# Linear attention before a mixture of experts: units of two heads of two sequences in place of four heads of one sequence with tails

## The chip, the core and the metric

The program runs on one core of a Trainium2 chip. TensorE (PE, with its weight loads listed apart as PEld) multiplies and transposes, VectorE (DVE) and ScalarE (ACT) do elementwise work and read PSUM, GpSimd (POOL) does elementwise work in SBUF and issues gathers, and the queue of SyncE (SP) issues most transfers. Each engine works through its own instructions in the order in which they were written down, and waits on semaphores. The metric is the device time of one execution in microseconds; lower is better. All arithmetic here is float32, which TensorE does in two passes, so that one matmul of the kernel is two records in the trace.

## What is computed

Attention without a softmax over pairs: `q` is normalised over its 64 features, `k` over the 576 positions, and a 64x64 matrix per head carries everything. Its output goes into a gated mixture of eight experts (two per token), and from there through a dense feed-forward layer.

```python
batch, n_heads, seq, head_dim = (4, 8, 576, 64)
q_s = softmax(q, axis=-1); k_s = softmax(k, axis=2)        # eps 1e-9 in the sums
kv = einsum('bhsd,bhse->bhde', k_s, v)
x = einsum('bhsd,bhde->bhse', q_s, kv)                     # -> (2304, 512)
logits = x @ w_gate
noisy = logits + log1p(exp(x @ w_noise)) * noise           # top 2 of 8 experts per token
out[token] += weight * (relu(x @ w1[e]) @ w2[e])           # 512 -> 1024 -> 512
h = out @ w_in; g = max(h, 0) + alpha * min(h, 0); result = g @ w_out
```

## The kernel before

The program has three stages: attention (to about 120 us), the experts, and the last layer. The second and third are one almost unbroken stream of matmuls, and the change leaves their code alone, but for which PSUM banks they share with attention and for the order of the output rows.

**Units.** Attention works in eight units. A unit is one sequence and four heads. Its first 512 positions lie on 128 partitions, four rows each (`"h (p c) d -> p h (c d)", c=4`), and so each run of memory in a load is 1 KB. The remaining 64 positions of each sequence are its tail. The tails of two sequences share one tile, one on each half of the partitions (`kt`, `vtr`, `qt`; runs of 256 bytes), and have instructions of their own: `k_tail`, `k_tail_exp`, a second part in `q_max`, `q_sub`, `q_exp`, `v_copy`, a fifth matmul in `kv_mm` (`et`, `vt`), and a third piece (`cc == 2`) of `q_tr`, `x_mm`, `x_out`.

**Steps of a unit.** `k_tree` (DVE) takes the maximum of `k` over a partition's rows, `k_tr` (PE) transposes that, `k_bc` reduces it over the partitions (DVE) and transposes the maximum back (PE), `k_row` (ACT) copies it to SBUF, `k_sub` (POOL; DVE for the first two units) subtracts, `k_exp` (ACT) takes the exponential. `q_max` (DVE), `q_sub` (POOL), `q_exp` (ACT) do the same for `q`. `v_copy` (POOL) puts a column of ones beside `v`. `kv_mm` (PE) multiplies, `kv_sum` (DVE, tile `rk`) and `kv_out` (ACT) normalise, `kv_tr` (PE and ACT, tile `kvt`) transposes the result and `kv_gate` multiplies it by the gate weights, so that the logits come out of the same matmul as the output. `q_tr` (PE, and ACT's copy to `qT`) transposes exp(q), `x_mm` (PE) multiplies into the PSUM tile `px`, `x_out` (DVE) normalises output and logits and sums the logits over the heads, `x_st` (SP) stores.

**Order.** Nothing reorders instructions. The loop `for t in range(-6, NU)` calls `slot(t)`, and a slot runs through the table `ORDER`: an entry `("kv_mm", 1)` does `kv_mm` of unit t+1. That table is the order of every engine's queue. Below, slot 0 is the one in which `x_mm` of unit 0 runs.

**Routing beside it.** The gate of the first half of the tokens (`gate`, a generator of some forty small DVE instructions with groups of PE matmuls in between) runs within slots 4 to 7: each `tick()` behind a DVE instruction of attention takes `TICKS[t]` steps of it. When it has ended, `fetch` puts four gathers of tokens (`xg`) into POOL's queue. `SPLITS` says at which entries of the table a piece of the first expert's weights is split into a high and a low part (`hi` on ACT, L165; `lo` on POOL, L166).

**The end of the stage.** In the last slot, at the entry `TURNED`, PE transposes two gathered blocks of tokens into PSUM tiles `pt`, ACT copies them to `xh`, and DVE forms `xl` from `pt` and `xh` at `SPLIT`. Then the first expert's matmuls begin (L755). Their accumulators take the banks `mm0` to `mm4` in turn, `mm0` first. Before, `pt` uses the banks `mm1` and `mm2`:

```python
for c, tag in enumerate(("mm1", "mm2")):
    pt = gps.tile([128, 4, 128], F32, name="pt", tag=tag)
```

Of the kernel before, what the change touches and what calls it, by code (L numbers as in the profile page):

```python
# [18 lines left out]
NT = 18  # L19
# [7 lines left out]
EPS = 1e-9  # L27
NVA = 2
NKV = 6
# [6 lines left out]
ORDER = [("k_tree", 3), ("x_mm0", 0), ("q_sub", 2), ("x_out0", 0), ("kv_mm", 1), ("k_tail", 2), ("k_exp", 2),  # L36
         ("kv_sum", 1), ("q_tr0", 1), ("k_tr", 3), ("x_mm2", 0), ("x_mm1", 0), ("k_bc", 3), ("kv_out", 1),
         ("k_tail_exp", 2), ("x_out2", 0), ("kv_tr", 1), ("q_tr1", 1), ("k_row", 3), ("x_st2", 0),
         ("load_k", 5), ("kv_gate", 1), ("q_max", 3), ("q_exp", 2), ("v_copy", 3), ("k_sub", 3), ("x_out1", 0),
         ("x_st0", 0), ("x_st1", 0), ("q_tr2", 1), ("load_v", 4), ("load_q", 5)]  # L40
# [12 lines left out]
def attention_moe_ffn(ctx, tc, q, k, v, w_gate, w_noise, noise, w1, w2, w_in, w_out, alpha, out):  # L53
# [126 lines left out]
    def attention():  # L180

        with ExitStack() as cx:
# [12 lines left out]
            vt = [att.tile([128, H, D + 1], F32, name=f"vt{i}") for i in range(2)]

            def main_src(a, b, g):
                return a[b, 4 * g:4 * g + 4, 0:512, :].rearrange("h (p c) d -> p h (c d)", c=4)

            def load(a, b, g, name):  # L200
                t = loads.tile([128, 4, 4, D], F32, name=name, bufs=3)
                nc.sync.dma_start(t.rearrange("p h c d -> p h (c d)"), main_src(a, b, g))
                return t
# [917 lines left out]
```

## Time and profile before

| | us |
|---|---|
| median of 3 runs (lowest, highest) | 995.41 (993.7, 996.4) |
| time of the profiled execution | 998.39 |
| its span, first to last instruction | 996.6 |
| PE busy, weight loads busy | 953.0, 860.0 |
| DVE, ACT, POOL busy | 508.0, 317.3, 307.0 |

A busy share is a mean over stages. PE is busy for 96% of the span, but for less in attention, and only there does it wait for others. To follow a change in attention, read the stretches of that stage (when the `x_mm` of each slot starts), and whether anything behind it has room. [...] The profiled execution is 3 us longer than the median, 1.8 us of its time lie outside the span.

### The profile page before, as it was taken

How to read it: one execution, taken by the hardware profiler on the slowest of the kernel's cores; microseconds unless marked ns; L12 is line 12 of the kernel's file. 1: busy time of each engine (PE TensorE's matmuls, PEld its weight loads, DVE VectorE, ACT ScalarE, POOL GpSimd, SP SyncE). 2: the span in 40 equal slices, each digit the busy share in tenths (PEclk: the TensorE clock that was granted, in tenths of full speed). 3: DMA queues.
4: the chain of work that ended last, by engine and by line, in shares of the span. 5: the costliest groups of instructions: out<-in, count | busy, mean ns of one | idle time of the engine just before them, and what ended most of it. 6: DMA issues, size and time to landing. Idle time of an engine off the chain costs nothing. (4 is left out here: it accounts for less than half of the span.)

```text
span 996.6 us, 14925 instructions
## 1 busy us (share of the span) xinstructions
PE 953.0 (96%) x5882; PEld 860.0 (86%) x5882; DVE 508.0 (51%) x1005; ACT 317.3 (32%) x603; POOL 307.0 (31%) x333
## 2 busy tenths in 40 slices
PE   4876799999999999999999999999999999999998
PEld 3765689998989898898988998989898989989896
DVE  6777563666757666666623354425161524334150
ACT  3554423433334333333333343212121222212120
POOL 6662730022212231312100127533251424323140
PEclk9986799999999999999999999999999999999999
DMA  9871643657656675756444262310101010100000
GB/s 251 247 215 54 213 146 124 191 164 239 192 184 205 181 240 162 244 171 200 149 136 136 81 200 70 88 51 14 53 15 61 15 50 22 43 22 11 11 12 21
DMA packets 65168, 121.77 MB, mean 122 GB/s; under 512 B 13488, under 2 KB 30400, under 8 KB 65088
## 3 DMA queue, kind: packets, MB, share of 16 engines
q1 hardware_dynamic: 49120, 83.98, 28.0%
q0 software_dynamic: 6080, 19.67, 6.4%
q10 hardware_dynamic: 9888, 17.08, 4.6%
q8 instruction: 48, 0.79, 0.3%
q14 instruction: 32, 0.26, 0.1%
HBM read 92.65 MB, written 28.05 MB: 121 GB/s over the span
## 5 line engine op out<-in xcount | busy, mean ns | idle before, releaser
L755 PE MATMUL mm<-xh,hi 128*128 128x256 f32 (+1 forms) x1088 | 318.4, 293 | 1.6 <-PEq L1080 0.9
L755 PE MATMUL mm<-xh,lo 128*128 128x256 f32 (+1 forms) x1088 | 318.3, 293 | 0.0
L755 PE MATMUL mm<-xl,hi 128*128 128x256 f32 (+1 forms) x1088 | 318.3, 293 | 0.0
L755 PEld LDWEIGHTS mm<-xh,hi 128*128 128x128 f32 x1088 | 205.8, 189 | 3.2 <-issue 1.3
L755 PEld LDWEIGHTS mm<-xl,hi 128*128 128x128 f32 x1088 | 205.3, 189 | 0.8
L755 PEld LDWEIGHTS mm<-xh,lo 128*128 128x128 f32 x1088 | 205.0, 189 | 0.0
L943 POOL TENSOR_TENSOR gl<-neg,gh 128x256 fp32r<-128x256 f32 x144 | 107.3, 750 | 166.1 <-ACT gh L942 164.8
L166 DVE TENSOR_TENSOR lo<-raw,hi 128x1024 fp32r<-128x1024 f32 x69 | 84.5, 1229 | 107.5 <-ACT hi L165 106.9
L940 DVE TENSOR_SCALAR neg<-mm,alph 128x256 f32<-128x256 f32 x144 | 69.2, 482 | 126.7 <-PE mm L755 124.7
L755 PE MATMUL mm<-hi,hh 128*128 128x512 f32 (+1 forms) x320 | 129.1, 403 | 0.0
L755 PE MATMUL mm<-hi,hl 128*128 128x512 f32 (+1 forms) x320 | 125.8, 393 | 0.0
L755 PE MATMUL mm<-lo,hh 128*128 128x512 f32 (+1 forms) x320 | 125.8, 393 | 0.0
L833 POOL TENSOR_TENSOR cva<-cva,raw 128x512 int32<-128x512 int32 x32 | 43.9, 1371 | 235.1 <-DVE raw L831 137.2
L755 PE MATMUL mm<-hi,gh 128*128 128x512 f32 x288 | 113.6, 394 | 0.0
L755 PE MATMUL mm<-hi,gl 128*128 128x512 f32 x288 | 112.3, 390 | 0.0
L755 PE MATMUL mm<-lo,gh 128*128 128x512 f32 x288 | 112.1, 389 | 0.0
L942 ACT CAST gh<-neg 128x256 fp32r<-128x256 f32 x144 | 57.6, 406 | 126.8 <-DVE neg L941 119.9
L780 ACT ACTIVATE hh<-mm 128x368 fp32r<-128x368 f32 (+1 forms) x128 | 54.9, 431 | 129.1 <-PE mm L755 119.7
L165 ACT CAST hi<-raw 128x1024 fp32r<-128x1024 f32 x80 | 83.2, 1047 | 28.0 <-DMA raw<-in_moe_w_dram 10.8
L781 DVE SCALAR_TENSOR_TENSOR hl<-mm,hh 128x368 fp32r<-128x368 f32 (+1 forms) x128 | 60.7, 479 | 57.8 <-ACT hh L780 57.4
L848 POOL DMA_INDIRECT xg<-ys,yidx x36 | 34.6, 962 | 157.8 <-DMA ys<-y 83.5
L709 DVE TENSOR_TENSOR xl<-pt,xh 128x512 fp32r<-128x512 f32 (+1 forms) x58 | 39.3, 678 | 69.2 <-ACT xh L706 68.9
(157 smaller groups left out, 1117.4 us busy)
## 6 DMA issues: line engine op xcount, KB each, us to landing
raw<-in_moe_w_dram SPq DMA_DIRECT2D x60, 512.0 KB, 3.9
ys<-y ACTq DMA_DIRECT2D x32, 256.0 KB, 2.0
raw<-in_moe_w_in_dram SPq DMA_DIRECT2D x16, 512.0 KB, 4.6
wc<-cvm SPq DMA_DIRECT2D x32, 256.0 KB, 4.9
raw<-in_moe_w_out_dram SPq DMA_DIRECT2D x16, 512.0 KB, 4.3
raw<-wc SPq DMA_DIRECT2D x16, 512.0 KB, 3.9
kr<-in_k_dram SPq DMA_DIRECT2D x8, 512.0 KB, 6.8
qr<-in_q_dram SPq DMA_DIRECT2D x8, 512.0 KB, 8.4
```

Source lines behind the costliest of these rows:

```text
L165: nc.scalar.copy(r(hi[:, sl]), raw)
L166: lo_eng.tensor_sub(r(lo[:, sl]), raw, hi[:, sl])
L709: nc.vector.tensor_sub(r(lo), pt, hi)
L755: nc.tensor.matmul(acc, r(a), r(b), start=(n, k) == steps[0], stop=(n, k) == steps[-1])
L780: nc.scalar.activation(r(hh[:, f, :]), acc[:, :n], AF.Relu)
L781: nc.vector.scalar_tensor_tensor(r(hl[:, f, :]), acc[:, :n], 0.0, hh[:, f, :], op0=OP.max, op1=OP.subtract)
L833: nc.gpsimd.tensor_tensor(a, a, low, op=OP.add)
L848: nc.gpsimd.indirect_dma_start(out=t, out_offset=None, in_=src, in_offset=bass.IndirectOffsetOnAxis(ap=yidx[:, i, T:T + 1], axis=0))
L940: nc.vector.tensor_scalar(t, a, 0.0, alph[:, f:f + 1], op0=OP.min, op1=OP.mult)
L942: nc.scalar.copy(r(GT[0][:, f, :]), t)
L943: nc.gpsimd.tensor_sub(r(GT[1][:, f, :]), t, GT[0][:, f, :])
```

## The change

A unit becomes two heads of two sequences. The sequence `2*hb` lies on partitions 0 to 63 and `2*hb + 1` on 64 to 127, with nine rows on each partition, 9 x 64 = 576. No tails remain. Runs of memory are 2304 bytes; a load is two transfers, one per half. There are again eight units.

- `kv_mm`: 18 matmuls a unit with 64 contraction rows each (two halves of nine rows), in place of 10 with 128 rows. The halves go to two PSUM banks.
- `x_mm`: 18 matmuls with 64 output partitions each, in place of 8 with 128 (and 4 with 64 in every second sequence), all into one tile `px` of three banks, of which there is one in place of two.
- `k_tr`, `k_bc`: two transposes a unit in place of six. The maximum is first spread by ACT (`kb`) and then transposed once.
- `x_out`: four DVE instructions a unit in place of five for each piece. `x_lg` sums the logits, on POOL, but for the last unit of each half of the tokens, where two adds are on DVE. `route` and its add fall away.
- `x_st`: three transfers of 384 KB every second unit.
- `ORDER`, `TICKS`, `SPLITS` are new; `kv_mm` stands one unit further ahead (2 in place of 1), `load_v` too. `pt` of the turned blocks uses `mm0` and `mm1`.
- `kv` has three buffers in place of six; noise is loaded in four transfers in place of eight; `out_rows` follows the new order of tokens.

```diff
-TICKS = {4: 1, 5: 2, 7: 3}
-SPLITS = {4: {"load_q": 1}, 5: {"load_q": 1}, 6: {"kv_mm": 1, "x_out1": 1, "load_q": 1},
-          7: {"kv_mm": 1, "x_out1": 1, "load_q": 1}}
+ORDER = [("x_mm", 0), ("k_tree", 3), ("k_exp", 2), ("q_sub", 2), ("kv_tr", 1), ("x_out", 0), ("q_tr0", 1), ("k_tr", 3),
+         ("kv_gate", 1), ("kv_mm", 2), ("k_bc", 3), ("q_tr1", 1), ("kv_sum", 2), ("k_row", 3), ("kv_out", 2),
+         ("load_k", 5), ("v_copy", 3), ("q_tr2", 1), ("q_max", 3), ("q_exp", 2), ("k_sub", 3), ("x_lg", 0),
+         ("x_st", 0), ("load_v", 5), ("load_q", 5)]
+TICKS = {4: 2, 5: 3, 6: 3, 7: 3}
+SPLITS = {4: {"load_q": 1}, 5: {"load_q": 1}, 6: {"kv_tr": 1, "k_bc": 1, "load_q": 1},
+          7: {"kv_tr": 1, "k_bc": 1, "load_q": 1}}
-TURNED, SPLIT = "x_st2", "load_q"
+TURNED, SPLIT = "kv_mm", "load_q"
...
+                t = loads.tile([128, 2, R * D], F32, name=name, bufs=3)
+                for u in range(2):
+                    nc.sync.dma_start(t[halves[u]], a[2 * hb + u, 2 * g:2 * g + 2].rearrange("h (p c) d -> p h (c d)", c=R))
...
+                kb = att.tile([128, 2, 64], F32, name="kb", bufs=2)
+                nc.scalar.copy(kb, km[:, :, None].to_broadcast([128, 2, 64]))
+                nc.tensor.transpose(pk[i][:, 1, :], kb.rearrange("p u n -> p (u n)"), ident)
...
+                p = pkv[i] = ps.tile([128, 2, 512], F32, name="pkv")
+                e = ek.pop(i)
+                for c in range(R):
+                    for u, h in enumerate(halves):
+                        nc.tensor.matmul(p[:, u, 0:130], e[h, c, :], va[i % NVA][h, :, c, :],
+                                         start=(c == 0), stop=(c == R - 1))
...
+                for c in range(R):
+                    for u, h in enumerate(halves):
+                        nc.tensor.matmul(px[i][h, c // 3, c % 3, :], t[:, c, h], m[:, u, :], start=True, stop=True)
...
-                nc.vector.reduce_sum(lgp[:, T:T + n, g, :], lt.rearrange("p c h n -> p c n h"), axis=AX.X)
...
+            def x_lg(i):
+                hb, g = divmod(i, G)
+                lt, at = lts.pop(i), lg[:, hb * R:(hb + 1) * R, :]
+                eng = nc.vector if g == G - 1 else nc.gpsimd
+                eng.tensor_add(at, lt[:, :, 0, :] if g == 0 else at, lt[:, :, int(g == 0), :])
+                if g:
+                    eng.tensor_add(at, at, lt[:, :, 1, :])
...
-                            for c, tag in enumerate(("mm1", "mm2")):
+                            for c, tag in enumerate(("mm0", "mm1")):
```

PE's queue in slot 1, from its first `x_mm` (`px`) to the last row ahead of the next slot's; `pkv` is `kv_mm`, `pq` is `q_tr`, `pk` are `k_tr` and `k_bc`, `bank` are `kv_tr` and `kv_gate`. Before (its `kv_132` is that of the unit of the slot):

```order
L395 MATMUL px<-kv_132,qT 128x162 x4
L332 MATMUL pkv<-va_141,ek 128x130 x4
L334 MATMUL pkv<-vt_143,et_139 128x130
L332 MATMUL pkv<-va_141,ek 128x130 x4
L334 MATMUL pkv<-vt_143,et_139 128x130
L379 MATMUL pq<-ident,eq 128x128 x4
L254 MATMUL pk<-ident,kt 128x128 x2
L256 MATMUL pk<-ident,m_436 128x128 x2
L395 MATMUL px<-kv_132,qT 128x162 x4
L265 MATMUL pk<-ident,km 128x128 x2
L357 MATMUL bank<-ident,kv_133 128x128 x2
L379 MATMUL pq<-ident,eq 128x128 x4
```

The same slot now (`kv_131` is that of its unit):

```order
L320 MATMUL px<-kv_131,qT 64x162 x18
L291 MATMUL bank<-ident,kv_132 128x128 x2
L310 MATMUL pq<-ident,eq 128x128 x3
L225 MATMUL pk<-ident,m_456 128x128
L298 MATMUL bank<-wg,kvt 128x16 x2
L271 MATMUL pkv<-va_134,ek 128x130 x18
L233 MATMUL pk<-ident,kb 128x128
L310 MATMUL pq<-ident,eq 128x128 x6
```

Before, a second `x_mm`, of the other two rows of the unit, stood between `kv_mm` and the next slot's first; now `x_mm` is one block, `kv_mm` stands behind `kv_tr` and `kv_gate`, and between it and the next `x_mm` PE has one transpose and six of `q_tr`.

DVE's queue at the end of the stage, from the last `x_out` on. Before:

```order
L408 TENSOR_TENSOR x<-px,rq_1238 128x512
L413 TENSOR_TENSOR lt_1243<-px,rq_1238 128x128
L417 TENSOR_REDUCE lgp<-lt_1243 128x2x16
L709 TENSOR_TENSOR xl<-pt,xh 128x4x128 x2
L478 TENSOR_TENSOR lg<-lgp 128x144
```

Now:

```order
L332 TENSOR_TENSOR x<-px,rq 128x9x128
L338 TENSOR_TENSOR lt<-px,rq 128x288
L347 TENSOR_TENSOR lg<-lg,lt 128x144
L349 TENSOR_TENSOR lg<-lg,lt 128x144
L625 TENSOR_TENSOR xl<-pt,xh 128x4x128 x2
```

The add of the logits stood behind `xl`, and two adds stand ahead of it now.

POOL's queue in the last two slots, now (`lo` are pieces of the first expert's weights, `xg` the gathers, `lg` the `x_lg` of unit 6):

```order
L166 TENSOR_TENSOR lo_886<-raw,hi_885 128x1024 x2
L604 DMA xg<-xs,tok_106 128x512 x4
L166 TENSOR_TENSOR lo_886<-raw,hi_885 128x1024
L347 TENSOR_TENSOR lg<-lg,lt 128x144
L349 TENSOR_TENSOR lg<-lg,lt 128x144
L166 TENSOR_TENSOR lo_1141<-raw,hi_1140 128x1024 x4
```

Before, four pieces stood between the last `et` and the gathers, and three behind them. Now two pieces stand ahead of the gathers, and the two adds of unit 6 stand behind the third.

## Rows read from the trace of the kernel before

**Rows 1.** Busy time by stretch; columns: stretch, its length, busy time per engine, PEclk, DMA share, GB/s
```profile
24.50:66.60 42.10, 34.78 (x244) 31.31 (x244) 28.98 (x69) 23.92 (x56) 26.43 (x20) 0.92 0.90 257
66.60:79.40 12.80, 8.35 (x57) 7.41 (x57) 12.47 (x33) 6.33 (x16) 7.31 (x6) 0.92 0.26 84
79.40:98.00 18.60, 11.93 (x90) 10.84 (x90) 11.89 (x38) 7.76 (x16) 6.97 (x4) 0.68 0.10 34
98.00:120.20 22.20, 16.05 (x94) 13.36 (x93) 13.18 (x47) 9.98 (x19) 15.44 (x9) 0.73 0.76 233
120.20:996.60 876.40, 870.90 (x5349) 789.15 (x5349) 426.22 (x804) 260.18 (x481) 235.22 (x254) 1.00 0.35 112
```

**Rows 2.** PE by time: start, length, line, tiles, records, idle before and releaser
```profile
15.88 1.94 PE L332 MATMUL pkv<-va,ek 128*128 128x130 f32 x8
...
38.37 0.38 PE L256 MATMUL pk<-ident,m 128*128 128x128 f32 x2
38.59 1.27 PE L395 MATMUL px<-kv,qT 128*128 128x162 f32 x8
39.70 0.38 PE L265 MATMUL pk<-ident,km 128*128 128x128 f32 x2
...
43.48 1.05 PE L332 MATMUL pkv<-va,ek 128*128 128x130 f32 x8
44.37 0.39 PE L334 MATMUL pkv<-vt,et 128*128 128x130 f32 x2
...
117.21 2.27 PE L705 MATMUL pt<-ident,xg 128*128 128x128 f32 x8 [2.73 <-DMA xg<-xs,tok]
120.15 1.23 PE L755 MATMUL mm<-xh,hi 128*128 128x256 f32 x4 [0.68 <-ACT xh L706]
```

**Rows 3.** POOL by time: a copy of `v`, and the first gather
```profile
46.68 1.04 POOL L319 COPY va<-vr 128x1024 f32<-128x1024 f32 x1 [7.67 <-DMA vr<-in_v_dram]
...
113.19 1.14 POOL L688 DMA_INDIRECT xg<-xs,tok  x1 [0.18 <-issue]
```

**Rows 4.** All engines by time in slot 5
```profile
81.78 2.35 POOL L166 TENSOR_TENSOR lo<-raw,hi 128x1024 fp32r<-128x1024 f32 x1 [0.33 <-ACT hi L165]
...
82.09 2.13 DVE L565 TENSOR_TENSOR gu<-gnl,gm 128x72 f32<-128x72 f32 x1
84.09 1.90 POOL L304 TENSOR_TENSOR eq<-qr,qm 128x1024 f32<-128x1024 f32 x1
84.25 1.82 DVE L567 TENSOR_TENSOR gu<-gu,rev 128x72 f32<-128x72 f32 x1
...
87.67 0.22 PE L581 MATMUL bank<-mask,tri 128*128 128x72 f16 x1 [5.70 <-DVE mask L576]
```

**Rows 5.** DVE by time: an add of logits with POOL idle
```profile
120.74 0.30 DVE L478 TENSOR_TENSOR lg<-lgp 128x144 f32<-128x144 f32 x1
```

**Rows 6.** DVE by form, 0 to 120 us; columns: shapes, count, busy us, mean ns, idle before
```profile
L244 DVE TENSOR_REDUCE m<-kr 128x256 f32<-128x1024 f32 x8 | 15.5, 1940 | 5.5 <-DMA kr<-in_k_dram 5.5
L408 DVE TENSOR_TENSOR x<-px,rq 128x512 f32<-128x512 f32 x16 | 11.0, 688 | 0.6 <-DMA xs<-x 0.2
L274 DVE TENSOR_REDUCE qm<-qr 128x16 f32<-128x1024 f32 x8 | 9.7, 1209 | 0.0
```

**Rows 7.** Weight loads of PE by time: 64 columns wide, then 128
```profile
62.41 0.47 PEld L395 LDWEIGHTS px<-kv,qT 128*64 128x64 f32 x8 [0.17 <-issue]
63.11 1.13 PEld L395 LDWEIGHTS px<-kv,qT 128*128 128x128 f32 x8 [0.23 <-issue]
```

**Rows 8.** ACT by form, 0 to 120 us
```profile
L350 ACT ACTIVATE kv<-pkv,rk 64x64 f32<-64x64 f32 x32 | 9.9, 309 | 1.8 <-DVE rk L341 1.4
L381 ACT COPY qT<-pq 128x512 f32<-128x512 f32 x16 | 9.4, 585 | 17.0 <-PE pq L379 16.5
```

**Rows 9.** POOL by form, 0 to 120 us
```profile
L285 POOL TENSOR_TENSOR ek<-kr,ks 128x1024 f32<-128x1024 f32 x6 | 14.2, 2374 | 10.1 <-ACT ks L269 7.8 <-DVE m L244 1.6 <-DMA nz<-in_moe_noise_dram 0.6
L291 POOL TENSOR_TENSOR et<-kt,ks 64x256 f32<-64x256 f32 x8 | 5.8, 723 | 0.3
```

More of the change, by code (lines that the diff above doesn't have):

```diff
@@ L27 @@
 EPS = 1e-9
+R = S // 64
 NVA = 2
-NKV = 6
+NKV = 3
 TG = 2
@@ L195, in attention @@
[L195 to L202, printed above, removed]
-                return t
-            def tail(a, hb, name):
-                t = loads.tile([128, H, D], F32, name=name, bufs=2 if name == "kt" else 1)
-                for u in range(2):
-                    nc.sync.dma_start(t[u * 64:(u + 1) * 64],
-                                      a[2 * hb + u, :, 512:576, :].rearrange("h p d -> p h d"))
-                return t
@@ L398, in x_out @@
-            def x_out(i, cc):
-                b, g = units[i]
-                T = 9 * (b // 2) + (8 if cc == 2 else 4 * (b % 2) + 2 * cc)
-                p, n = px.pop((i, cc)), 1 if cc == 2 else 2
-                rq = att.tile([128, n, 2, 2], F32, name=f"rq{n}", bufs=3)
+                m, t, p = kv[i % NKV], kvt.pop(i), bank[:, 256:288].rearrange("p (u n) -> p u n", u=2)
+                for u in range(2):
+                    nc.tensor.matmul(p[:, u, :], t[:, u, :], wg[:, i % G, :], start=True, stop=True)
@@ L440, in small_loads @@
                 for b in range(B):
-                    T, u = 9 * (b // 2) + 4 * (b % 2), b % 2
-                    nc.sync.dma_start(nz[:, T:T + 4, :],
-                                      noise[b * S:b * S + 512].rearrange("(p c) e -> p c e", c=4))
-                    nc.sync.dma_start(nz[u * 64:(u + 1) * 64, 9 * (b // 2) + 8, :],
-                                      noise[b * S + 512:(b + 1) * S])
-                nc.sync.dma_start(al, alpha.rearrange("(c p) -> c p", p=128))
-            def thirds(fn):
-                return [lambda i, cc=cc: (cc < 2 or units[i][0] % 2) and fn(i, cc) for cc in range(3)]
-            ops = {f.__name__: f for f in (load_k, load_q, load_v, v_copy, k_tree, k_tr, k_bc, k_row, k_sub, k_tail,
-                                           k_exp, k_tail_exp, q_max, q_sub, q_exp, kv_mm, kv_sum, kv_out, kv_tr,
-                                           kv_gate)}
-            for name, fn in (("q_tr", q_tr), ("x_mm", x_mm), ("x_out", x_out), ("x_st", x_store)):
-                ops.update((f"{name}{cc}", f) for cc, f in enumerate(thirds(fn)))
+                    nc.sync.dma_start(nz[halves[b % 2], b // 2 * R:(b // 2 + 1) * R, :],
+                                      noise[b * S:(b + 1) * S].rearrange("(p c) e -> p c e", c=R))
+                nc.sync.dma_start(al, alpha.rearrange("(c p) -> c p", p=128))
+            ops = {f.__name__: f for f in (load_k, load_q, load_v, v_copy, k_tree, k_tr, k_bc, k_row, k_sub, k_exp,
+                                           q_max, q_sub, q_exp, kv_mm, kv_sum, kv_out, kv_tr, kv_gate, x_mm, x_out,
+                                           x_lg, x_st)}
+            ops.update((f"q_tr{t}", lambda i, t=t: q_tr(i, t)) for t in range(3))
             def slot(t):
@@ L506, in attention @@
                 load_piece(queue=nc.scalar)
-            second = route(9, NT)
+            second = gate(R, NT)
             next(second)
```

244 lines of the change are left out of this document (80 added, 164 removed).

## The prediction

> **What bounds the kernel now.** I read the busy times by stretch first [rows 1]. From 120.2 us to the end PE is busy for 870.9 of 876.4 us at full clock. The change leaves that work alone, so the tail moves as a block with its first matmul, and what I have to predict is when the first expert matmul (L755) starts: now at 120.15 us [rows 2]. In front of it PE is never full: 34.8 of 42.1 us in slots 0 to 3, 8.35 of 12.8 in slot 4, 11.9 of 18.6 in slot 5, 16.05 of 22.2 from slot 6 to the expert matmul, and the clock granted to it falls to 0.68 and 0.73 in the last two. Reducing work on an engine helps only where PE waits for it.
>
> PE by time [rows 2] shows what one step costs and where PE waits at the end: the transposes of the gathered tokens (L705) stood idle for 2.73 us until the gather landed, 4.02 us after it was issued at 113.19 [rows 3]. POOL by time shows the waits for transfers: a copy of `v` waited 7.67 us [rows 3]. The third view is slot 5, all engines by time [rows 4]. There PE's gate matmul waits 5.70 us for DVE's mask, and it stands ahead of `kv_mm` in PE's queue. The mask's steps are small, 128x72, but took 2.13 and 1.82 us, each to the end of a POOL instruction (81.78 + 2.35 = 84.13 and 82.09 + 2.13 = 84.22; 84.09 + 1.90 = 85.99 and 84.25 + 1.82 = 86.07). A larger DVE add took 0.30 us with POOL idle [rows 5]. So DVE instructions that work in SBUF alone stand still here beside large POOL instructions. That matters, since the change puts new ones there.
>
> **The change part by part.** All times are on the profiled execution's scale: 998.39 us, 3.0 above the median of 995.41. I subtract the same difference from either.
>
> *Start, to the first `x_mm` (24.55 us now): +5.2.* `kv_mm` of unit 0 now stands ahead of `k_bc` of unit 1 in PE's queue, and a second `kv_mm` ahead of the first `x_mm`. Before any of this the clock is low: eight `kv_mm` records took 1.94 us at 15.88 [rows 2]. The 36 records of unit 0 at about 0.1 to 0.14 us end near 18. Behind them come, on ACT and DVE, the copy `ks`, `q_max` (1.21), `k_sub` (taken as long as `q_max`, since it reads as much) and `k_tree` (1.94) [rows 6]; then `k_tr` of unit 2 near 22.4, `kv_gate` 0.55, `kv_mm` of unit 1 about 4 us at mixed clock, and the 2.9 us of latency below: 29.8. `k` arrives without its tails, perhaps 1.5 us earlier (an estimate from four fewer small transfers), which is already in it.
>
> *Slots 0 to 3 (42.1 us now, 10.5 each): -4.3.* The period becomes one pass of PE's queue with one uncovered wait.
> - `x_mm`: 36 records. 128 columns wide, eight take 38.59 to 39.70, 0.139 each [rows 2]. Half as wide, eight take 62.41 to 63.11, 0.0875 each, of which the loads are 0.47 / 8 = 0.059 [rows 7]. I take 0.08, near the measured pace, a little less because the two halves alternate: 2.88 us.
> - `kv_tr`, three blocks of `q_tr`, `k_tr`: six transposes. Two take 38.37 to 38.59, so 0.11 each: 0.65 us. `kv_gate`: four records at 0.139: 0.55 us.
> - `kv_mm`: 36 records. Eight with all 128 rows take 43.48 to 44.37, 0.111 each [rows 2]. The trace of before has no matmul on 64 rows, so the bounds are 0.111 (halves one after another, 4.0 us) and 0.111 x 0.059 / 0.139 = 0.047 (halves side by side, only limited by loading; 1.7 us). I take 0.111 x 0.08 / 0.139 = 0.064, 2.3 us, because the nearest measured row of a half tile [rows 7] gave 0.63 of the full one.
> - Wait of PE between its last `q_tr` and `x_mm`, with nothing behind to fill it: transposes 0.43, copy `qT` 0.48, copy `ks` 0.28, `kv_out` 4 x 0.31, copy `qT` 0.48 (both copies scaled from 0.585 for four blocks [rows 8]): 2.9 us. With 0.16 for `k_bc`: 9.45 a slot, 37.8 for four.
>
> The waits for loads go: runs of 2304 bytes replace 1 KB and 256 bytes, and `load_v` stands one slot earlier. If they don't, the price is the 7.67 us of rows 3, for one slot; POOL's `v_copy` would hold up `k_sub` behind it.
>
> [...] Rows 7 agree that fewer columns load faster; no row shows a load of half the rows.
>
> *Slot 4 (12.8): +0.1.* It has as many `kv_mm` as before, and no large wait goes. The two adds of `x_lg` of unit 3 are on DVE and stand behind POOL's `k_sub` and `q_sub`, ahead of `k_tree` of unit 7; the gate gets 2 steps per tick in place of 1.
>
> *Slot 5 (18.6): -2.0.* More of the gate has run before it, but the mask still meets a `lo` of 2.35 us and `q_sub` of 1.90 [rows 4], and `kv_mm` of unit 7 still waits behind the gate matmuls. 16.5 is the old length less one of the two stalled steps.
>
> *Slot 6 to the first expert matmul (22.2): -3.7.* There is no `kv_mm` left in slot 6; the gathers stand behind two `lo` pieces in place of four, 7 us into the slot, and take the same 4.0 us to the transposes [rows 2, 3]. Then POOL runs a `lo` (2.37, as the one of rows 4 and `k_sub` of rows 9) and the two adds of unit 6, at 0.55 each (an estimate, from 0.72 for half the partitions and 256 elements a row [rows 9]). A new wait arises. Block 0 of `pt` sits in `mm0`, and that is the bank of the first expert accumulator; until now the first expert matmul waited only for ACT's `xh` [rows 2]. Now it waits for DVE's `xl`. Ahead of `xl` in DVE's queue are the two adds of unit 7, which wait for POOL's adds of unit 6 and then run beside a new `lo`. Behind that matmul is PE's whole remaining stream. With one add stalled the stretch is 18.5 us, with both 20.9. I take 18.5: an add is 0.30 without disturbance [rows 5], and in rows 4 a stall ended with the POOL instruction, so that the second add may slip in between.
>
> *At nothing.* `x_out` goes from 100 DVE instructions to 32 and loses some 11 us (16 of 0.688 [rows 6] become fewer and longer ones); `k_bc` shrinks. In slots 0 to 3 DVE is busy for 29.0 of 42.1 us [rows 1] and is not what PE waits for last, so this gain lies beside ACT's chain. If that cover went, `k_tree` and the two `rk` steps would come sooner by at most 2 us a slot. POOL loses `et` (8 x 0.72) and gains `k_sub`, `q_sub`, `v_copy` that are an eighth longer and ten adds: about even. ACT gains `kb` and loses the tail's exponentials: even; it is busy for 23.9 of 42.1 us. Stores of 384 KB go beside the loads that the slot waits for no more.
>
> Sum: 5.2 - 4.3 + 0.1 - 2.0 - 3.7 = -4.7; rounded to -4.5, 993.9 for a profiled execution, 991 for the median (995.4 - 4.5 = 990.9).
>
> **The rivals.**
> *The halves run one after another (other side, slower).* `kv_mm` keeps 0.111 per record: 4.0 in place of 2.3 us. It stands on PE's path in six slots (units 2 to 7: +10.2) and at the start (+1.3): 995.4 - 4.5 + 11.5 = 1002.4. It decides from 0.082 us per record on: 4.5 us over seven units of 36. For it: 36 records replace 20 and each loads 128 columns [rows 2]. Against: the narrower tile of rows 7 did gain. [...]
> *Side by side at the pace of the loads.* `x_mm` 36 x 0.059 = 2.1 and `kv_mm` 1.7: 1.36 less in each of six slots, 1.0 less at the end: -9.2 more, 982. For it: 0.47 of the 0.70 us in rows 7 is loading. Against: no row reaches that pace.
> *DVE's adds stand still beside POOL.* Both adds of unit 7 wait for a `lo` each (+2.4), and both of unit 3 for `k_sub` or `q_sub`, with the gate's extra steps (+2.2 in slot 4): the gain is gone, 995.5. For it: rows 4. Against: a stalled step starts again between two POOL instructions.
> *It doesn't do what it says:* less DVE work is off the path anyway; that is in the sum at nothing.
>
> **How the numbers follow.** A measurement here tells about 0.3% (3 us) from no change. Chances: forecast (986 to 997) 0.45, one after another 0.25 (998 to 1008), side by side 0.15 (976 to 985), stalled adds 0.15 (992 to 999). Faster: 0.33 + 0.14 + 0.01 = 0.48. Same: 0.09 + 0.01 + 0.09 + 0.01 = 0.20. Slower: 0.03 + 0.24 + 0.05 = 0.32, the last for stalls that go further. 978 to 1003 leaves out half of the slow rival, a sixth of the quick one and little else. The forecast's own range is 986 to 997.
>
> **What would show it.** The pace of `kv_mm` (L271) in slots 1 to 3: 0.064 forecast, 0.111 and 0.047 the rivals; that of `x_mm` (L320): 0.08. The start of `x_mm` in slots 0 to 7: 29.8, then every 9.45 to slot 4 at 67.6. In front of `x_mm` an idle PE of some 2 us, released by ACT's `qT`. Waits for `vr` absent from POOL. In slot 5 the idle time before the gate matmul (5.70 now), about 4. At the end, the releaser of the first matmul of L671: DVE's `xl` (L625) and not ACT's `xh`; and the length of the adds (L347, L349) on DVE: 0.3 or some 2 us. I am wrong if slot 0 begins past 32 us, if a load ends the waits, or if another engine than PE with ACT's copies sets the slot's period.

## The result and the profile after

The changed kernel took 1001.58 us (median of 13 runs, 999.49 to 1010.46) against 995.41 us of the kernel before (13 runs, 993.7 to 998.72): 1.0069 of its time, 95% interval 1.0049 to 1.0090. It is 0.7% slower, clear of the spread of its runs, where 991 and faster was forecast. Timed once more beside later experiments it was at 1.0039 (1.0027 to 1.0052); the two timings of one kernel differ by 0.3%, so a step of an experiment under 0.3% is not read as one here. The ratios, not the times, are compared between experiments: the kernel before took from 995.4 to 997.8 us in the series that they were timed in.

Busy time by stretch, as in [rows 1]: slots 0 to 3, slot 4, slot 5, slot 6 to the first expert matmul, the rest. Columns: stretch, its length, busy time of PE, weight loads, DVE, ACT, POOL, granted clock as a share of full speed (PEclk), DMA share, GB/s.

```profile
33.10:66.60 33.50, 29.57 (x358) 25.49 (x356) 24.64 (x37) 23.27 (x57) 25.68 (x18) 1.00 1.01 245
66.60:83.60 17.00, 11.24 (x93) 9.41 (x91) 14.36 (x29) 6.88 (x19) 6.57 (x4) 0.67 0.65 173
83.60:101.60 18.00, 13.46 (x125) 11.45 (x124) 12.57 (x32) 6.79 (x14) 7.83 (x6) 0.69 0.28 96
101.60:125.40 23.80, 13.22 (x97) 10.51 (x96) 12.88 (x21) 11.70 (x18) 19.83 (x13) 0.72 0.61 204
125.40:1005.90 880.50, 872.47 (x5349) 790.71 (x5349) 427.14 (x803) 258.48 (x479) 231.59 (x252) 0.99 0.36 111
```

This profile is of a long execution (1007.72 us). A second one of the same kernel (999.5 us), from the later timing, stands beside it in the table, so that what varies can be told from what is always there. The last column is the kernel before with 46 small matmuls of no use at its start (an experiment below); its attention is the same program:

| us | before | forecast | after | after, again | before, padded |
|---|---|---|---|---|---|
| first `x_mm` | 24.5 | 29.8 | 33.1 | 32.7 | 25.3 |
| slots 0 to 3 | 42.1 | 37.8 | 33.5 | 33.5 | 38.7 |
| slot 4 | 12.8 | 12.9 | 17.0 | 17.1 | 12.9 |
| slot 5 | 18.6 | 16.5 | 18.0 | 14.8 | 19.8 |
| slot 6 to first expert matmul | 22.2 | 18.5 | 23.8 | 21.6 | 21.1 |
| first expert matmul at | 120.2 | 115.5 | 125.4 | 119.7 | 117.8 |
| from there to the end | 876.4 | 876.4 | 880.5 | 878.0 | 878.4 |

Slots 0 to 3 gain. The start, slot 4 and what stands behind the first expert matmul cost in both profiles; slot 5 and the end differ between the two. The two profiles of the kernel before differ by 3.4 us in slots 0 to 3. In the first, POOL waited 7.67 us for a load of `v` [rows 3], and PE then 3.75 us in slot 2; in the second the two waits are 5.54 and 1.64:

```profile
52.72 0.33 PE L357 MATMUL bank<-ident,kv 128*128 128x128 f32 x1 [3.75 <-ACT kv L350]
```

So the gain of slots 0 to 3 is 5.2 to 8.6 us, by the execution that it is measured against. PE by time, after (rows as in [rows 2]): `x_mm` and `kv_mm` in slot 1, then where PE waits in slot 4 and at the end of attention.

```profile
41.50 2.70 PE L320 MATMUL px<-kv,qT 128*64 128x162 f32 x36
45.95 2.28 PE L271 MATMUL pkv<-va,ek 64*128 64x130 f32 x36
...
73.42 0.48 PE L225 MATMUL pk<-ident,m 128*128 128x128 f32 x1 [3.39 <-DVE m L220]
75.70 1.04 PE L298 MATMUL bank<-wg,kvt 128*128 128x16 f32 x4 [1.80 <-ACT kvt L293]
76.67 4.27 PE L271 MATMUL pkv<-va,ek 64*128 64x130 f32 x36
...
117.41 1.09 PE L621 MATMUL pt<-ident,xg 128*128 128x128 f32 x8
125.40 1.19 PE L671 MATMUL mm<-xh,hi 128*128 128x256 f32 x4 [6.89 <-DVE xl L625]
```

ACT makes the last copy for that `x_mm` while it runs:

```profile
42.32 0.48 ACT L311 COPY qT<-pq 128x384 f32<-128x384 f32 x1
```

`kv_mm` runs at 2.28 / 36 = 0.063 us a record, `x_mm` at 0.075. In slot 4 PE waits twice, and the same `kv_mm` takes 4.27 us there, with a granted clock of 0.50 from 76.6 to 81.0 us, behind these waits; it was 1.00 for the 2.28 us in slot 1. At the end PE waits 6.89 us for `xl`. Behind this wait and the first one of slot 4 stand adds of logits on DVE; DVE and POOL by time:

```profile
66.36 2.67 POOL L248 TENSOR_TENSOR ek<-kr,ks 128x1152 f32<-128x1152 f32 x1 [1.50 <-ACT ks L237]
66.70 2.49 DVE L347 TENSOR_TENSOR lg<-lg,lt 128x144 f32<-128x144 f32 x1
68.98 2.19 POOL L256 TENSOR_TENSOR eq<-qr,qm 128x1152 f32<-128x1152 f32 x1
69.23 2.10 DVE L349 TENSOR_TENSOR lg<-lg,lt 128x144 f32<-128x144 f32 x1
71.26 2.11 DVE L220 TENSOR_REDUCE m<-kr 128x128 f32<-128x1152 f32 x1
...
119.87 2.41 DVE L347 TENSOR_TENSOR lg<-lg,lt 128x144 f32<-128x144 f32 x1
122.32 2.33 DVE L349 TENSOR_TENSOR lg<-lg,lt 128x144 f32<-128x144 f32 x1
124.57 1.28 DVE L625 TENSOR_TENSOR xl<-pt,xh 128x512 fp32r<-128x512 f32 x2
```

As in [rows 4], each add ends with the POOL instruction beside it: 66.36 + 2.67 = 69.03 and 66.70 + 2.49 = 69.19; 68.98 + 2.19 = 71.17 and 69.23 + 2.10 = 71.33.

The adds are not all of the end. The transposes of the gathered tokens (117.41) began 15.8 us behind the start of slot 6, 15.4 in the second profile, where the forecast had 11 (7 to the gathers, 4.0 for the gather). The gathers were issued in time (109.21), but PE was still at `x_mm` of unit 7. That had waited for ACT's copy to `qT`, which stood in ACT's queue behind a `hi`, and that waited for weights. ACT, then PE:

```profile
110.50 1.04 ACT L165 CAST hi<-raw 128x1024 fp32r<-128x1024 f32 x1 [1.97 <-DMA raw<-in_moe_w_dram]
111.57 0.48 ACT L311 COPY qT<-pq 128x384 f32<-128x384 f32 x1
...
112.11 0.90 PE L310 MATMUL pq<-ident,eq 128*128 128x128 f32 x3 [3.55 <-ACT qT L311]
112.94 4.55 PE L320 MATMUL px<-kv,qT 128*64 128x162 f32 x36
```

The granted clock was 0.63 from 101.6 to 117.4 us, and this `x_mm` took 4.55 us in place of 2.70.

### The profile page after: what moved, and what is told of

It reads as the page before. It is cut to its first block, busy times and chain, and to the rows that moved or that the text cites. A ratio compares the mean times of both kernels' runs of the same rounds, so it can differ in the third digit from the quotient of the medians.

```text
span 1005.9 us, 15295 instructions
## 1 busy us (share of the span) xinstructions
PE 953.5 (95%) x6106; PEld 858.6 (85%) x6106; DVE 507.0 (50%) x937; ACT 316.5 (31%) x605; POOL 305.6 (30%) x316
```

## Experiments on the adds

**The last unit's adds behind `xl`.**

```diff
+                    if name == "x_lg" and t == NU - 1:
+                        continue
...
+            x_lg(NU - 1)
             extra_cx.close()
```

> The two logits adds of the last unit (L347, L349) are issued behind xl instead of ahead of it; nothing else changes. Theory (the adds, standing still beside POOL's lo pieces for 2.41 and 2.33 us, are what xl and so the first expert matmul wait for): first expert matmul about 1 us behind ACT's first xh, 119.5 to 120.5 us where it was 125.40, PE's wait there 1 to 2 us instead of 6.89, time 1001.6 - 5 = 996.5. Rival (something else is just as late: xl itself stands still beside lo, or the matmuls starve on hi and lo behind it): first matmul past 123 us, or the gain lost in the next 30 us, time 1000 to 1002.

Measured: 1000.75 us, ratio 1.0049 (1.0031 to 1.0067). The first expert matmul came at 117.62 us, but 10.5 us later PE waited 3.17 us for `hl`. DVE:

```profile
117.98 1.90 DVE L347 TENSOR_TENSOR lg<-lg,lt 128x144 f32<-128x144 f32 x1
119.92 2.39 DVE L349 TENSOR_TENSOR lg<-lg,lt 128x144 f32<-128x144 f32 x1
122.34 2.32 DVE L452 SCALAR_TENSOR_TENSOR ga<-lg 128x72 f32<-128x72 f32 x1
```

The adds and the gate's first step stand beside four `lo` in a row on POOL and hold up DVE in this place too. The matmul started even before the 119.5 to 120.5 us of the theory; the gain was given back, as the rival said.

**Unit 3's adds behind `k_bc`.** In slot 3 `x_lg(3)` is called right behind `k_bc` instead of behind `k_sub`.

> The two logits adds of unit 3 move in DVE's queue from behind q_max (where they ran 2.49 and 2.10 us beside POOL's k_sub and q_sub, ahead of k_tree of unit 7) to right behind k_bc, where DVE waits for kv_mm and POOL runs only a copy of v. Theory (those adds hold up k_tree and with it k_tr, k_exp and kv_mm of slot 4): adds 0.3 to 0.5 us each, PE's wait of 3.39 us for k_tree gone, slot 4 shorter by 3 to 4.5 us (17.0 to about 13), time 1001.6 - 4 = 997.5. Rival (ACT's gate exponential and k_exp, or the low clock, take up the room): slot 4 at 15.5 us or more, time 1000 or more.

Measured: 1000.66 us, 1.0046 (1.0029 to 1.0062). The adds took 0.54 and 1.13 us and delayed nobody; slot 4 went from 17.0 to 15.0 us, not to 13. DVE of this run has a new releaser:

```profile
70.22 2.12 DVE L220 TENSOR_REDUCE m<-kr 128x128 f32<-128x1152 f32 x1 [3.27 <-DMA kr<-in_k_dram]
```

So the adds hid a load of `k` that was as late as they were. The waits of SP's queue from 40 to 76 us in the kernel after (second profile; columns: who waited, for what, us, times, longest) say why:

```profile
SPq L205 <- DMA raw<-in_moe_w_dram: 8.0, 1, 8.0
SPq L205 <- DMA qr<-in_q_dram: 2.9, 3, 2.2
```

The second half of `k` of unit 7 was issued 8 us late. The profile names as releaser a load of expert weights (`raw`) that ACT had issued; from this is inferred that the one transfer waited for the other, and the next run puts it to the test. In the kernel before that wait (5.0 us there) held up a store.

**That weight load one slot later**, on top of the last run (`if t == 3` becomes `if t == 4` ahead of the two `load_piece`).

> The run with unit 3's adds moved (e2), and the first two loads of expert weights are issued one slot later (at slot 4 instead of slot 3). In e2 k_tree of unit 7 waited 3.27 us for k of unit 7, whose second transfer SP issued 8 us late, behind one of those weight loads. Theory (in slot 4 the adds and that load hide each other): with both gone k_tree starts at about 67 instead of 70.2 us, PE's wait for k_tr is gone, slot 4 falls from 15.0 to about 12.5 us and the time by 2.5 us against e2: ratio 1.002. Rival (the slot is held by the transfers as such, which are busy throughout slots 0 to 3): k_tree starts after 69.5, ratio 1.004 to 1.005 as e2.

Measured: 997.42 us, 0.9996 (0.9982 to 1.0010), 0.5% less than without it. `k_tree` of unit 7 starts at 67.89 us, slot 4 takes 13.6 us. The theory holds: two causes hid each other, and the pair brings the gain. That the later load alone would not is argued and was not run: the adds end at 71.33 us on DVE wherever the load stands. The slots of one profile don't carry this alone, as slot 4 differs by 2 to 3 us between profiles of one attention program (12.7 and 15.8 us in two runs further down); the timing does. What is left of slot 4's wait is ACT's `kvt` (2.83 us).

**`lo` of slots 6 and 7 on DVE.**

```diff
-                        split_piece(*pieces.pop(0), nc.gpsimd, False)
+                        split_piece(*pieces.pop(0), nc.vector if t > 5 else nc.gpsimd, False)
```

> The low parts (lo) of the first expert's weights in slots 6 and 7 are computed on DVE instead of POOL; nothing else. Theory (DVE's logits adds and small steps stand still beside POOL's lo, and the gathers stand behind lo in POOL's queue): adds of the last unit 0.3 us each instead of 2.41 and 2.33, first gather at about 102 to 104 instead of 109 us, first expert matmul at 116 to 118 us without a wait for hl behind it, time 1001.6 - 4 = 997.5. Rival (DVE as the new bound: it waits for ACT's hi and the weights' loads in its own order, ahead of x_out): first expert matmul past 121, time 1001 or more.

Measured: 1001.01 us, 1.0033 (1.0020 to 1.0047); the first expert matmul at 121.53 us, with 4.18 us of waiting for `xl`. DVE:

```profile
118.99 1.23 DVE L166 TENSOR_TENSOR lo<-raw,hi 128x1024 fp32r<-128x1024 f32 x1 [0.39 <-ACT hi L165]
120.13 0.30 DVE L347 TENSOR_TENSOR lg<-lg,lt 128x144 f32<-128x144 f32 x1
120.47 0.31 DVE L349 TENSOR_TENSOR lg<-lg,lt 128x144 f32<-128x144 f32 x1
120.70 1.28 DVE L625 TENSOR_TENSOR xl<-pt,xh 128x512 fp32r<-128x512 f32 x2
```

With POOL free of `lo` the adds take 0.30 us, which shows the cause of their 2.4. Little of the time is gained, because DVE's own order (`x_out`, `lo`, adds, `xl`) now stands ahead of `xl`: the rival.

## Experiments on the rest of the program

The forecast let everything behind the first expert matmul move as a block. It doesn't: 876.4 us before, 878.0 and 880.5 after. Most of the difference appears at one place, at the first tokens of the last layer, where the program branches past code for experts that overflow (not taken with these inputs). PE by time there, in the kernel before:

```profile
630.67 0.36 PE L755 MATMUL mm<-xh,hi 128*128 128x256 f32 x1 [0.92 <-PEq L1080]
```

In the kernel after:

```profile
636.07 0.35 PE L671 MATMUL mm<-xh,hi 128*128 128x256 f32 x1 [1.33 <-PEq L993]
639.08 0.37 PE L671 MATMUL mm<-xl,hi 128*128 128x256 f32 x1 [1.59 <-issue]
```

Both stop for the branch itself. After the change PE stops again 3 us on. The second stop, of 1.04 to 1.64 us, stands in all nine profiles of the kernel after and of versions with as many PE instructions, and not in that of the kernel before. No engine or transfer is named. The change adds 441 PE instructions ahead of the branch target (a count of the compiled programs, not of a trace). That the target's position in PE's program sets the stop is an assumption so far; two runs move it, by amounts that the author chose from such counts.

**64 more PE instructions at the start**: 16 matmuls of one column, while PE has nothing to do. If the position sets the second stop, the stop can go here.

```diff
     make_identity(nc, ident)
+    for _ in range(16):
+        nc.tensor.matmul(bank[0:1, 0:1], ident[:, 0:1], ident[:, 0:1], start=True, stop=True)
```

> Changed kernel with 16 matmuls of one column at the very start, which add 64 instructions to PE's program while PE has nothing to do; everything else the same. [...] Rival (the stop is data or a wait that the trace doesn't show): it stays, time 1001 to 1002.

**The kernel before with 46 such matmuls** (the same lines with `range(46)`).

> Kernel before with 46 matmuls of one column at the very start, which add 184 instructions to PE's program; nothing else. [...] Theory (position in PE's program): the second stop of about 1.6 us appears 3 us behind the branch at about 633 us, time 995.8 + 2.5 = 998.3. Rival (the stop belongs to the new attention or the new row order): no stop, time 995 to 996.5.

PE by time at the branch, in the padded kernel after:

```profile
631.50 0.36 PE L673 MATMUL mm<-xh,hi 128*128 128x256 f32 x1 [1.93 <-PEq L995]
```

In the padded kernel before:

```profile
628.52 0.35 PE L757 MATMUL mm<-xh,hi 128*128 128x256 f32 x1 [0.74 <-PEq L1082]
631.58 0.39 PE L757 MATMUL mm<-xh,lo 128*128 128x256 f32 x1 [1.52 <-issue]
```

The second stop goes with the position and comes with it: it stands in ten profiles, these nine and the padded kernel before, and in none of the ten others, seven of them of versions with 64 PE instructions more. Measured: 998.87 us, 1.0014 (1.0001 to 1.0028) for the first, 0.25 to 0.55% below the two timings of the kernel after; 999.10 us, 1.0015 (1.0003 to 1.0027) for the second, 0.15% or 1.5 us more than the kernel before beside it, where 2.5 us were expected. Both steps are near the 0.3% that is read as one, so the price in time is less firm than the stop.

The price depends on the granted clock too. Busy time in the 6 us behind the branch, columns as above (the clock is the third from the right): the kernel after, again, and padded:

```profile
636.00:642.00 6.00, 4.34 (x24) 4.28 (x25) 0.91 (x2) 1.36 (x3) 0.63 (x1) 0.75 0.21 49
629.50:635.50 6.00, 4.57 (x37) 4.51 (x38) 2.10 (x5) 1.62 (x4) 0.74 (x1) 1.00 0.21 49
631.50:637.50 6.00, 6.00 (x38) 6.00 (x39) 2.16 (x5) 1.60 (x4) 0.73 (x1) 0.72 0.20 46
```

Matmul by matmul against the kernel before (clock 1.00 there), PE loses 1.6 to 2.0 us in this place in the profiles with the second stop and clock 1.00, and 2.9 to 4.7 in those with it and a clock of 0.63 to 0.75. The padded kernel after has no second stop, but lost 2.5 us with clock 0.72 and a first stop of 1.93; so its own profile does not show the gain that its timing shows. Why the clock falls in some executions stays open. So does what PE waits for in the second stop: 10 or 11 matmuls, with a weight load each, run between the two stops, and the trace names no releaser for the second (`issue`, 1.59 us in the kernel after).

The rest is the last store: an output tile is now two stores on ACT's queue, one for each half. ACT's queue at the end, after:

```profile
1002.05 1.12 ACTq L880 DMA_DIRECT2D out_dram<-y  x2
```

From its start to the end of the span are 1005.9 - 1002.05 = 3.85 us. Before, one store took 0.34 us of issue, at 993.42, and 3.18 us remained: 0.67 less.

## Experiments on the start and on the halves

**Halves one after another.** In `kv_mm` and `x_mm` the two loops are exchanged, so that nine matmuls of one half stand in a row.

```diff
-                for c in range(R):
-                    for u, h in enumerate(halves):
+                for u, h in enumerate(halves):
+                    for c in range(R):
```

> The 18 matmuls of kv_mm and of x_mm are issued half by half (nine of the lower half, then nine of the upper) instead of in turn; same matmuls, same count. Theory (neighbouring matmuls on different halves of the array overlap, and the pace of 0.063 us a record comes from that): kv_mm of slots 1 to 3 goes from 2.28 to about 4.0 us (0.111 a record), x_mm from 2.70 to 3.2 (0.0875) or more. Rival (a half tile is quicker by itself, whatever stands beside it): 2.28 and 2.70 stay within 0.2.

Measured in a single execution: 1034.31 us, some 33 more than the kernel after. PE by time in slot 1:

```profile
52.89 4.67 PE L320 MATMUL px<-kv,qT 128*64 128x162 f32 x36
...
58.99 3.95 PE L271 MATMUL pkv<-va,ek 64*128 64x130 f32 x36
```

3.95 / 36 = 0.110, the pace of a matmul with all 128 rows (0.111, [rows 2]), and 0.130 for `x_mm` (0.139 at full size). The granted clock was 1.00 there. A half tile by itself is hardly quicker; neighbours on different halves overlap. Slots 0 to 3 took 47.7 us here, against 33.5 with halves in turn and 38.7 to 42.1 before the change: without the alternation the change would lose there.

**Order at the start.** Ahead of slot 0 `kv_mm`, `kv_sum` and `kv_out` stand behind `k_sub` in the table.

> Only before slot 0: kv_mm, rk and kv_out stand behind k_bc, q_max and k_sub of the next unit in the order, so that the transposes of the maxima no longer wait for 4.27 us of kv_mm at the low clock. Theory (PE's order at the start costs it): first x_mm at about 30 instead of 33.1 us, slots behind it unchanged, time 1001.6 - 3 = 998.6. Rival (the loads of units 1 and 2, or POOL's 3.16 us q_sub, set the start): first x_mm stays within 1 us of 33.1, time 1001 to 1002.

Measured: 1001.04 us, 1.0050 (1.0033 to 1.0068), the first `x_mm` at 34.13. DVE no longer waits for PE's `kv_mm` (3.92 and 4.61 us at 21.02 and 31.56 in the kernel after), but now for loads:

```profile
20.09 1.35 DVE L241 TENSOR_REDUCE qm<-qr 128x18 f32<-128x1152 f32 x1 [2.87 <-DMA qr<-in_q_dram]
...
23.64 2.20 DVE L220 TENSOR_REDUCE m<-kr 128x128 f32<-128x1152 f32 x1 [0.66 <-DMA kr<-in_k_dram]
```

The transpose of unit 2 came at 25.98 us in place of 26.18, and `kv_mm` of unit 1 now stands directly ahead of the first `x_mm`, which came 1 us later than in the kernel after. The rival holds in so far as PE's order alone gains nothing: the loads are about as late as the order, though their runs had become longer. The next runs ask why.

**The kernel before with loads in partition halves**, and **in head pairs**. Each load becomes two, either of 64 partitions or of two heads on all 128; 256 KB and runs of 1 KB in both.

```diff
-                nc.sync.dma_start(t.rearrange("p h c d -> p h (c d)"), main_src(a, b, g))
+                for u in range(2):
+                    hs = slice(u * 64, (u + 1) * 64)
+                    nc.sync.dma_start(t[hs].rearrange("p h c d -> p h (c d)"), main_src(a, b, g)[hs])
```

> Kernel before with each load of q, k and v made as two transfers of 64 partitions, runs of 1 KB as they were; nothing else. From 6 to 30 us the kernel before moved 281 GB/s at a DMA share of 1.09, the changed kernel 208 GB/s at 1.00. Theory (two transfers of half the partitions are slower than one of all): the stretch falls to 200 to 230 GB/s at a full share, and the first x_mm comes 2 to 5 us later than 24.55. Rival (it is the run of 2304 bytes, or the layout of the rows): 265 GB/s or more at a full share, first x_mm within 1 us.

> Kernel before with each load of q, k and v made as two transfers of two heads each, on all 128 partitions, runs of 1 KB; the same number and size of transfers as in the run with partition halves (f1: 186 GB/s at a full share, first x_mm at 32.6 us, 1012 us). Theory (half of the partitions is what is slow): 6 to 30 us at 265 GB/s or more at a full share, first x_mm within 1.5 us of 24.55, time 995 to 999. Rival (twice the number of transfers of half the size): 180 to 220 GB/s, first x_mm past 29, time over 1005.

**The kernel after with loads by head**: again two transfers of 288 KB, but each of one head on all 128 partitions (`t[:, h, :]` from `"u (p c) d -> u p (c d)"`).

> The changed kernel with nothing but the loads split by head instead of by partition half: same number, size and runs of transfers, all 128 partitions in each. Theory: 6 to 30 us at 250 GB/s or more instead of 208 at a full DMA share, first x_mm at 26 to 29 instead of 33, ratio 1.0039 to 1.0069 less 0.004 to 0.006, that is 0.999 to 1.002. Rival (start set by PE's order): first x_mm stays within 1.5 us, ratio 1.004 to 1.007.

> The combined version with the weight loads later (d2, ratio 0.9963), and each load of q, k and v split by head instead of by partition half: again two transfers of 288 KB with runs of 2304 bytes, but each on all 128 partitions. Theory (transfers on half the partitions set the start): 6 to 30 us at 250 to 280 GB/s, first x_mm at 27 to 29 us instead of 34.4, ratio 0.989 to 0.992. Rival (the start is set by kv_mm at the low clock and the order of PE): first x_mm within 1.5 us of 34, ratio 0.995 to 0.996.

Busy time from 6 to 30 us; the last three columns are granted clock, DMA share and GB/s. The kernel before:

```profile
6.00:30.00 24.00, 15.73 (x95) 13.11 (x96) 19.06 (x27) 10.21 (x20) 15.51 (x24) 1.00 1.09 281
```

The kernel after:

```profile
6.00:30.00 24.00, 10.97 (x74) 9.10 (x76) 13.78 (x15) 7.09 (x16) 9.75 (x5) 0.89 1.01 211
```

The kernel before with loads in halves:

```profile
6.00:30.00 24.00, 12.65 (x47) 8.96 (x46) 13.40 (x15) 5.83 (x11) 9.50 (x21) 1.00 1.01 186
```

The kernel before with loads in head pairs:

```profile
6.00:30.00 24.00, 14.49 (x77) 11.74 (x77) 17.91 (x23) 8.79 (x18) 13.32 (x23) 1.00 1.09 259
```

The kernel after with loads by head:

```profile
6.00:30.00 24.00, 0.92 (x2) 0.36 (x2) 2.48 (x3) 0.56 (x2) 1.14 (x1) 1.00 0.14 50
```

The kernel before was timed once with each kind of load. Halves make the kernel before 1012.4 us, with the first `x_mm` at 32.6 in place of 24.5; head pairs leave it at 996.6, with 26.9. That is 2.3 us for twice the transfers of half the size, more than the 1.5 expected, and 5.7 us on top for the 64 partitions. So it is mainly the partitions that cost: the DMA engines are busy throughout and move a quarter less (186 / 1.01 = 184 against 259 / 1.09 = 238 GB/s at a full share). Why 64 partitions move less, no run shows.

The loads by head failed, and tell nothing of the start: 1215.14 us (1.2184) and, with the combined version below, 1209.63 us (1.2131), the first of them at a DMA share of 0.14 and 50 GB/s from 6 to 30 us. The source's slowest dimension is the sequence, of size two; that this is the cause is not shown. Nor is it shown whether the changed kernel's start would be regained with transfers of all partitions: no run here has it with such transfers at full speed.

## Putting it together

**Combined**: `lo` of slots 6 and 7 on DVE, unit 3's adds early, the start's order, 64 PE instructions, the second store of a tile on SP's queue.

> Changed kernel with the low parts of slots 6 and 7 on DVE, the adds of unit 3 behind k_bc, the start's order with kv_mm late, 64 more PE instructions at the start, and the second of the two stores of an output tile on SP's queue. If the four losses are separate they add: 1001.6 - 4 (end of attention) - 1 (adds of unit 3, as measured) - 0.5 (start, as measured) - 2.5 (branch) - 0.7 (last store) = 993. If one wait takes over from another at the end of attention: 996 to 998.

Measured: 996.88 us, 1.0001 (0.9989 to 1.0013). The rest behind the first expert matmul is 876.4 us, that of the kernel before. The first `x_mm` stayed at 34.4 to 34.6 us in the combined versions, so the start's order gained nothing here either, and the ratio is that of the second expectation, in which one wait takes over from another.

**With the weight loads one slot later.**

> The combined version (b4, ratio 1.000) with the two weight loads one slot later. Theory as in d1: 2 to 2.5 us less, ratio 0.9975. Rival: ratio 1.000, because the weights' high and low parts then come later and the first expert matmul waits for them.

Measured: 994.08 us, 0.9963 (0.9947 to 0.9978): faster than both kernels. Slot 4 takes 11.4 us and has clock 1.00 again, and the first expert matmul starts at 115.54. The forecast's 115.5 is met by chance: the parts are 34.4 to the first `x_mm`, then 33.4, 11.4, 14.8 and 21.5 us, where it had 29.8, 37.8, 12.9, 16.5 and 18.5. Slot 4:

```profile
67.80:79.20 11.40, 7.61 (x91) 6.49 (x90) 10.76 (x26) 6.45 (x17) 5.99 (x4) 1.00 0.68 230
```

**`xl` ahead of the last `x_out`** (`TURNED, SPLIT = "kv_tr", "x_out"`), without and with the later weight loads.

> The combined version (b4) with the two gathered blocks transposed right behind x_mm of the last unit and xl ahead of x_out of that unit in DVE's queue (it stood behind x_out, a lo and the adds, and the first expert matmul waited 4.18 us for it). Theory (at the end of attention it is now DVE's order alone that counts): first expert matmul about 1.5 to 2 us behind the transposes, near 114 instead of 117.1 us, and 2.5 to 3 us off the time: 0.997 of the kernel before where b4 was 1.000. Rival (PE then waits as long for the banks that x_out of the last unit empties, or for hi and lo): the first matmul comes earlier and the same time is lost within the next 15 us, ratio 0.999 to 1.000.

> c1 (xl ahead of the last x_out, ratio 1.000, where the first expert matmul waited 3.62 us for a high part) with the two weight loads one slot later. If the loads of k and not the weights set the end: ratio 0.9975 like d2. If the weights' path (load, hi, lo) sets the end there: first expert matmul later than in c1, ratio 1.000 or more.

Measured: 997.44 us, 1.0000 (0.9990 to 1.0011), and 995.28 us, 0.9976 (0.9962 to 0.9990). Nothing is gained by it: the first expert matmul at 119.17 then has another releaser, the rival's.

```profile
119.17 0.71 PE L682 MATMUL mm<-xh,hi 128*128 128x256 f32 x4 [3.62 <-ACT hi L167]
```

**The gate's first steps later** (no step at `k_tree` of slot 4, three a tick there), on top of the first of these, and **the kernel after** itself beside them.

> c1, and the first steps of the gate no longer stand at k_tree of slot 4, where ACT's exponential of the gate (waiting for DVE's ga behind k_tree) stood ahead of k_exp and kvt; three steps a tick in that slot instead of two. Theory: PE's wait of 2.34 us for kvt in slot 4 is gone, slot 4 12.65 to about 10.5 us, ratio another 0.002 below c1. Rival (the gate's mask ends last in slot 5): slot 4 shorter, slot 5 longer by the same, ratio as c1.

> The changed kernel itself beside the others on one chip, to compare them directly: ratio to the kernel before 1.0049 to 1.009 as at first; the second stop of some 1.6 us behind the branch is there; slots 0 to 3 take 33.5 us.

Measured: 1003.48 us, 1.0074 (1.0061 to 1.0087), against 1.0000 without it; the kernel after 999.91 us, 1.0039, less than the 1.0049 to 1.0090 expected, with slots 0 to 3 and the second stop as expected. The wait for `kvt` is gone, and the gate's matmuls now stand in PE's queue in slot 4, ahead of `x_mm`; PE waits there for `kb`, and for DVE's `base_h`:

```profile
79.21 0.33 PE L235 MATMUL pk<-ident,kb 128*128 128x128 f32 x1 [3.32 <-ACT kb L234]
...
85.49 0.28 PE L424 MATMUL bank<-ident,al 16*128 16x16 f32 x1 [3.15 <-DVE base_h L533]
```

Slot 4 became 17.7 us (15.8 in the run without it) and slot 5 18.3 (14.9). The larger part is in slot 5, where the rival had put it, though more than it had: there PE waits 3.74 us for DVE's `gplace`, another step of the gate. Neither had foreseen a longer slot 4 from the gate's own matmuls, moved ahead.

## Why the prediction was wrong, step by step

- **"The tail moves as a block": wrong**, by 1.6 to 4.1 us. It took the code as untouched and left out where it lies. Matmul by matmul PE runs up to 0.8 us ahead of the kernel before as far as the branch, and loses 1.7 and 3.7 us there. Two runs show the branch's second stop as a matter of position; the granted clock behind the branch, which varies, is the rest of it. The last store adds 0.67 us by the trace.
- **Start, +5.2: mis-sized**, measured +8.6 and +8.2. The order of PE was named as the cause; loads turned out to be about as late, and another order alone gains nothing. "`k` arrives perhaps 1.5 us earlier" took longer runs for faster loads; in the trace `k_tree` of unit 0 started at 6.12 us in place of 6.51, and from 6 to 30 us the transfers moved 211 GB/s in place of 281. The clock taken as low at 15.88 us was granted at 1.00 in the trace of the kernel before, though eight records took 1.94 us; of the two `kv_mm` of 4.27 us at the start of the kernel after, the first had 1.00 (16.70 us) and the second 0.51 (27.24 us). In the kernel before, loads in halves cost 8.1 us there, 5.7 of them by the 64 partitions.
- **Slots 0 to 3, -4.3: right in mechanism, too small**, measured -8.6 against the profile that it started from and -5.2 against the second one. Some 3.4 us of the 42.1 were that execution's own: the forecast counted them as gained, and then took off the 3.0 us by which that execution exceeds the median. How much of the 3.0 lies in these slots, and so was counted twice, no run shows. `kv_mm` is the 0.064 of the forecast, `x_mm` 0.075 in place of 0.08. (0.08 is 0.58 of a full record's 0.139, not the 0.63 of the text.) What was mis-sized is the uncovered wait: 2.9 us in the sum, while in slot 1 PE is idle for 0.57 us before `q_tr2` and 0.40 before `kv_gate`. The sum laid `ks`, `kv_out` and the last copy `qT` end to end ahead of `x_mm`; in the trace `x_mm` starts at 41.50 us on the first copies, and `kv_out` and the last copy (42.32) run beside it. The period is 8.37 us. The price stands in the next slots: loads fill the DMA engines (share 1.01) at 245 GB/s, and the load of unit 7 is late.
- **Slot 4, +0.1: wrong**, +4.2 and +4.3. The adds behind POOL were named in it and priced at next to nothing; they took 4.6 us ahead of `k_tree`. Beneath them lay the late load, which no step named, and the forecast's own list had "if a load ends the waits" as a sign of being wrong. Another of its signs came true too, slot 0 past 32 us; and a wait of POOL for `vr`, which was to be gone, stands at 74.73 us with 3.56 us.
- **Slot 5, -2.0**: measured -0.6 and -3.8. The second is the rule: ten further profiles of changed versions have 14.8 to 15.2 us there. The wait before the gate matmul (5.70 before) was 3.27 and 1.51 us, so in the second about two stalled steps went, where the forecast had one.
- **End, -3.7: the wrong bound taken**, measured +1.6 and -0.6. The new wait of the first expert matmul for `xl` was named, and so were its ends, 18.5 with one add stalled and 20.9 with both. It took 18.5; both adds stalled in the first profile (2.41 and 2.33), one and a part in the second (0.64 and 2.34). The rows cited [rows 4] had shown both steps stalled. But even the 20.9 was passed: the transposes came 4 us later than the gathers allowed, by the chain from the weights over ACT's `hi` and `qT` to `x_mm` of unit 7, and no step of the forecast had that.
- **The rivals.** "One after another", the slow one with 0.25, is refuted as a mechanism (0.063 us a record), though its 1002 is the time that came: luck. "Side by side at the pace of the loads" had 0.047 and 0.059, which no row reached. "Stalled adds" named one of the mechanisms and gave 995.5 for it alone. Some 2 to 4 us more came from outside the stage.

## What to carry to other kernels

Matmuls that alternate between the two halves of the array overlapped here (0.063 us a record, 0.110 half by half), and a unit split that way can be worth the shorter tiles; but don't count on longer runs of memory where a load is cut to 64 partitions for them (211 GB/s in place of 281 here), and time a load with a dimension of two outermost before it is kept (50 GB/s here). Where a change lengthens or shortens an engine's program ahead of a branch, look at that branch in both traces (a second stop of 1.04 to 1.64 us here). A releaser shown in a trace can hide a second that ends 1 us earlier: cost both, and try them together. Before a wait in one profile is counted as a gain, see whether a second execution has it.

## What was not expected of the hardware

- Loads in transfers of 64 partitions: 186 GB/s at a DMA share of 1.01, where the same bytes in transfers of 128 partitions moved 259 at 1.09; 50 GB/s at 0.14 where the outermost dimension was two.
- Position of a branch target in PE's program: a second stop of 1.04 to 1.64 us, with none of the work changed.
- A transfer of one queue can wait for another queue's: 8.0 us of SP for a load that ACT had issued. That it waited for that load is inferred from the releaser named; with the load one slot later the time fell by 0.5%.
- DVE adds in SBUF next to POOL: 2.1 to 2.5 us, to the end of the POOL instruction; 0.30 without one.
